# Gathers for experts 4 to 7 issued before the last store lands, and the weights of experts 6 and 7 loaded 1 MB at a time

## The chip, the cores and the metric

The kernel runs on one core of one Trainium2 chip. The metric is device time in microseconds (us), the median of several executions. Lower is better.

## The reference

The program is a linear attention followed by a mixture of experts with one expert per token. Cut to what matters:

```python
# q, k, v: (4, 8, 768, 64) float32;  gamma_h = 1 - 2 ** (-5 - h)
for t in range(S):
    state = gamma * state + outer(k[t], v[t])          # per batch and head
    y[t] = scale * q[t] @ state
x = y.transpose(0, 2, 1, 3).reshape(3072, 512)          # N tokens, D = 512
out = x
chosen = x @ w_skip > 0
e = argmax(x @ w_gate)                                  # one of 8 experts
y = softmax_weight * (relu(x @ w1[e]) @ w2[e])          # w1: 512 x 1024, w2: 1024 x 512
out[chosen] = x[chosen] + y[chosen]
```

All inputs and the output are float32. The kernel computes the expert products in bfloat16 and adds them up in float32.

## The kernel before

**Attention.** A loop over 16 pairs of heads, four for each of the four batches, computes the attention in chunked form (lines 540 to 610). The rows of batch b are put together in an SBUF tile `xall[b]`, which has two buffers, and stored to `out` in HBM. The last batch is stored in two steps, each on SP's and ACT's queue (lines 324 and 327). The gate of a batch (`g_logits` to `slots`) finds for each expert the tokens that go to it and writes their row numbers into slots. Slots 0 to 127 of every expert (s = 0, table `SL[0]`) are filled from batches 0 to 2 alone; slots 128 to 255 (s = 1, `SL[1]`) hold the rest and rows of the last batch.

**Experts.** A tile is a pair (e, s) of 128 tokens of one expert. For each tile the kernel does the following:
- `gather` (line 623): an indirect DMA on POOL reads the 128 rows out of `out` into a buffer `xg`, of which there are eight.
- `cast` (637): VectorE (DVE) casts them to bfloat16 (`xb`).
- `turn` (642): TensorE (PE) transposes them, and a copy brings them to SBUF (`xgT`).
- `layer1` (664): PE multiplies by `w1b[e]`, ACT applies the ReLU (`hT`).
- `second` (680): PE multiplies by `w2b[e]` into one of two PSUM buffers (`yps`).
- `give_back` (689): DVE computes `yo`, of which there are three buffers, and an indirect DMA on POOL scatters it to the rows of `out` (695).

**Weights.** `piece_w` (165) issues one piece of an expert's weights as a DMA on POOL, which casts from float32 to bfloat16: 512 KB read, 256 KB written, eight pieces per expert, `give(n)` issues the next n. Experts 0 to 4 have homes of their own and are loaded during the attention. The homes of experts 5 to 7 (pool `late`, line 718) take the place of the attention's tiles once these are released (717).

**Order.** All engines run the order written in the code. Each engine works its own list in order, so an instruction of POOL that waits holds up all that stands behind it, DMA issues included. After the attention, the first tiles of experts 0 to 3 are gathered (707), eight pieces of expert 5 are issued (722), and the first two tiles are computed while the gate of the last batch runs. Line 735 then gathers the second tiles of experts 0 to 3; these read rows of the last batch and wait for its store. From line 757 on, a loop goes over ten tasks: tiles (2,0), (3,0), (0,1) to (3,1) alone, then experts 4 to 7 with both tiles. In each round PE does layer 1 of task n, the transposes of task n + 1 and layer 2 of task n; DVE does the copy of n + 1, the cast of n + 2 and `yo` of n; POOL issues the scatters of n, then the gathers of `rows_of`, then pieces of `give`. After the scatters of round 6 POOL drains (769). A loop at the end (774) handles experts with more than 256 tokens and isn't entered with this input.

Of the kernel before, what the change touches and what calls it, by code (L numbers as in the profile page):

```python
# [9 lines left out]
FP32 = mybir.dt.float32  # L10
# [8 lines left out]
def kernel(  # L19
# [12 lines left out]
    PE, V_, A_, G_, SP = nc.tensor, nc.vector, nc.scalar, nc.gpsimd, nc.sync  # L32

    B, H, S, D = q.shape
    N, DM = out.shape
    E = moe_w1.shape[0]
# [10 lines left out]
    NST = CAP // 128  # L47
    NFIRST = 4
    NEARLY = 5
# [53 lines left out]
    for n in range(NIDLE):  # L103
        PE.matmul(
            out=idle[:, 0, :].rearrange("p (a c) -> p a c", a=4), lhsT=ones[:, :],
            rhs=ones[:, :].unsqueeze(1).to_broadcast([128, 4, 128]), start=True, stop=True,
# [34 lines left out]
    for r in range(R):  # L141
        for hi in range(2):
            G_.affine_select(
                out=maskc[64 * hi : 64 * hi + 64, r, :], in_=maskc[64 * hi : 64 * hi + 64, r, :],
# [14 lines left out]
    w1b, w2b = {}, {}  # L159

    def home_w(e, pl):
        w1b[e] = pl.tile([128, NDB, F], BF16, tag=f"w1_{e}", bufs=1, name="w1b")
        w2b[e] = pl.tile([128, NFB, DM], BF16, tag=f"w2_{e}", bufs=1, name="w2b")

    def piece_w(e, which, a):
        if which == 0:
            G_.dma_start(out=w1b[e][:, a, :], in_=moe_w1[e, a * 128 : (a + 1) * 128, :])  # L167
        else:
            G_.dma_start(  # L169
                out=w2b[e][:, 2 * a : 2 * a + 2, :].rearrange("p r d -> p (r d)"),  # L170
                in_=moe_w2[e, a * 256 : (a + 1) * 256, :].rearrange("(p r) d -> p (r d)", r=2),
            )
# [3 lines left out]
    pieces = [(e, w, a) for e in range(NEARLY) for w in range(2) for a in range(4)]  # L176

    def give(n):
        for _ in range(n):
            if pieces:  # L180
                piece_w(*pieces.pop(0))
# [179 lines left out]
    def g_turn(Gs):  # L361
        lp = wide("lps")
        for j in range(G):
            PE.transpose(out=lp[:, 0, j * 128 : (j + 1) * 128], in_=Gs[:, j * 128 : (j + 1) * 128], identity=ident[:, :])
        L = st("L", [128, NCH, 9])
        l4 = lp[:, 0, 0 : G * 128].rearrange("p (j c k e) -> p j c k e", j=G, c=2, k=2)
        half = st("half", [128, NCH, 9])
        V_.tensor_copy(half[:, :, :].rearrange("p (j c) e -> p j c e", c=2), l4[:, :, :, 0, 0:9])
        V_.tensor_tensor(
            out=L[:, :, :].rearrange("p (j c) e -> p j c e", c=2), in0=l4[:, :, :, 1, 0:9],  # L370
            in1=half[:, :, :].rearrange("p (j c) e -> p j c e", c=2), op=ALU.add,
        )
        return L
# [124 lines left out]
    gt, SL = {}, {}  # L498
# [41 lines left out]
    for i in range(NU + 1):  # L540
# [28 lines left out]
        if i == 1:  # L569

            identb = poolC.tile([128, 128], BF16, name="identb")
# [43 lines left out]
    poolE = ctx.enter_context(tc.tile_pool(name="esb", bufs=1, side="right", reuse_waits="tile"))  # L615
    xg, xgT, hTs = {}, {}, {}
    gathers, scatters = [], []

    def free_of(d, others):
        for o in others:  # L620
            tc.declare_no_dep(d.ins, o.ins, reason="the slots of a pass name distinct rows; rows of empty slots are not used")

    def gather(e, s, gi, upto, first=True):
        t = poolE.tile([128, DM], FP32, tag="xg", bufs=8, name="xg")
        d = G_.indirect_dma_start(  # L625
            out=t[:, :], out_offset=None, in_=out[0:upto, :],
            in_offset=bass.IndirectOffsetOnAxis(ap=gi[:, e : e + 1], axis=0), bounds_check=upto - 1, oob_is_err=False,
        )
        xg[e, s] = t
        if first:  # L630
            free_of(d, scatters)
            gathers.append(d)


    xbs = {}

    def cast(e, sts):
        for s in sts:
            xbs[e, s] = poolE.tile([128, DM], BF16, tag="xb", bufs=3, name="xb")
            V_.tensor_copy(xbs[e, s][:, :], xg[e, s][:, :])  # L640

    def turn(e, sts, copy=V_.tensor_copy):
        xgT[e] = poolE.tile([128, NDB, CAP], BF16, tag="xgT", bufs=3, name="xgT")
        for s in sts:
            ps = psum.tile([128, 2, 512], FP32, tag="P", bufs=2, name="xtp")
            pb = ps[:, 0, :].bitcast(BF16)
            for db in range(NDB):
                PE.transpose(
                    out=pb[:, db * 128 : (db + 1) * 128], in_=xbs[e, s][:, db * 128 : (db + 1) * 128], identity=identb[:, :]
                )  # L650
            copy(  # L651
                xgT[e][:, :, s * 128 : (s + 1) * 128], pb[:, 0 : NDB * 128].rearrange("p (a t) -> p a t", a=NDB)
            )

    tasks = [(2, [0]), (3, [0])] + [(e, [1]) for e in range(NFIRST)] + [(e, [0, 1]) for e in range(NFIRST, E)]
    todo = [(e, 1) for e in range(NFIRST)] + [(e, s) for e in range(NFIRST, E) for s in range(NST)]

    def rows_of(n):
        for _ in range(n):
            if todo:  # L660
                e, s = todo.pop(0)
                gather(e, s, SL[s][0], N)

    def layer1(e, sts):
        c0, n = sts[0] * 128, 128 * len(sts)
        hT = poolE.tile([128, NFB, CAP], BF16, tag="hT", bufs=2, name="hT")
        for f2 in range(NFB // 2):
            hp = psE.tile([128, 2, CAP], FP32, tag="hps", bufs=2, name="hps")
            for f in range(2):
                fb = 2 * f2 + f  # L670
                a, r = divmod(fb, 2)
                for db in range(NDB):
                    PE.matmul(  # L673
                        out=hp[:, f, 0:n], lhsT=w1b[e][:, db, a * 256 + r : (a + 1) * 256 : 2], rhs=xgT[e][:, db, c0 : c0 + n],
                        start=(db == 0), stop=(db == NDB - 1),
                    )
            A_.activation(out=hT[:, 2 * f2 : 2 * f2 + 2, 0:n], in_=hp[:, :, 0:n], func=AF.Relu, bias=0.0, scale=1.0)  # L677
        return hT
# [24 lines left out]
    def layer2(e, hT, sts, SL, first=False):  # L703
        for n, s in enumerate(sts):
            give_back(e, s, second(e, hT, n), SL, first)

    for e in range(NFIRST):
        gather(e, 0, SL[0][0], (B - 1) * S)
# [5 lines left out]
    Gs = g_cols(B - 1)  # L714
    t_x(NU - 1)
    turn(0, [0])
    stR.close()
    poolL = ctx.enter_context(tc.tile_pool(name="late", bufs=1, reuse_waits="tile"))
    for e in range(NEARLY, E):
        home_w(e, poolL)  # L720
    pieces += [(e, w, a) for e in range(NEARLY, E) for w in range(2) for a in range(4)]
    give(8)
    psE = ctx.enter_context(tc.tile_pool(name="pse", bufs=1, space=bass.MemoryType.PSUM, reuse_waits="tile"))
    L = g_turn(Gs)
    turn(1, [0])
    ha, pe = g_pick(L)
    h0 = layer1(0, [0])
    cp = g_count(B - 1, ha)
    g_vals(B - 1, ha, pe)
# [6 lines left out]
    cast(2, [0])  # L736
    give_back(0, 0, yp, SL, True)
    h0 = layer1(1, [0])
    turn(2, [0], A_.copy)
    cast(3, [0])  # L740
    layer2(1, h0, [0], SL, True)
# [4 lines left out]
    def passes():  # L746

        cn = g_count_all()
        top = poolC.tile([128, 1], FP32, name="top")
        V_.tensor_reduce(out=top[:, :], in_=cn[:, 0, 0:E], axis=AXX, op=ALU.max)  # L750
        V_.tensor_scalar(thr[:, :], thr[:, :], top[:, 0:1], None, ALU.is_lt)
        npass = poolC.tile([128, 1], FP32, name="npass")
        V_.tensor_reduce(out=npass[:, :], in_=thr[:, :], axis=AXX, op=ALU.add)
        V_.tensor_copy(npass_i[:, :], npass[:, :])

    give(4)
    for n, (e, sts) in enumerate(tasks):
        hT = layer1(e, sts)
        if n + 1 < len(tasks):
            turn(*tasks[n + 1])  # L760
        if n + 2 < len(tasks):
            cast(*tasks[n + 2])
        layer2(e, hT, sts, SL, True)
        rows_of(2 if n < 2 else 1)
        give(2)
        if n == 2:
            passes()
        if n == 6:
            G_.drain()
# [4 lines left out]
    with tc.For_i(0, n_more) as _:  # L774
        V_.tensor_scalar(posT[:, :], posT[:, :], -float(CAP), None, ALU.add)
        V_.memset(Tsb[:, :], 0.0)
        for b in range(B):
            slot_table(one_hots(poolE, chunks(b), every), chunks(b), every)
        SL2 = {s: slots(poolE, s, f"l{s}") for s in range(NST)}
        for e in range(E):  # L780
            for s in range(NST):
                gather(e, s, SL2[s][0], N, False)
            cast(e, [0, 1])
            turn(e, [0, 1])
            layer2(e, layer1(e, [0, 1]), [0, 1], SL2)
# [30 lines left out]
```

## Time and profile before

| | us |
|---|---|
| median of 3 runs | 221.69 |
| the runs | 222.35, 219.22, 221.69 |
| the profiled execution | 218.75 |
| its span, first to last instruction | 216.9 |

| engine | busy us | share of the span |
|---|---|---|
| PE, matmul | 190.7 | 88% |
| PE, weight load | 145.4 | 67% |
| POOL | 116.7 | 54% |
| DVE | 98.0 | 45% |
| ACT | 81.5 | 38% |

All times in the trace count from the first instruction. PE's matmul and weight load overlap and are listed apart. A hole is time in which an engine waits; the trace names what ended it. POOL's time for a DMA is that of its issue; the transfer lands later, and the time from issue to landing is listed by itself. The granted clock of PE was 0.992 of its full speed over the span, and 1.00 in every stretch of the experts' part up to the last product. DMA share is the mean busy share of the core's 16 DMA engines and can come out slightly over 1.

### The profile page before, as it was taken

The page shows a single profiled execution, that of the slowest core. Times are in us where ns is not written, and L with a number is a line of the kernel's source. Part 1 is how long each engine was busy: PE and PEld are TensorE (multiplying, and loading weights), DVE is VectorE, ACT ScalarE, POOL GpSimd, SP SyncE. Part 2 cuts the span into 40 slices and gives each one's busy share as a digit, 9 for nine tenths or more (in the row PEclk, how much of TensorE's full clock was granted, in tenths as well). Part 3 has the DMA queues.
Part 4 walks back from the last instruction along what each step waited for, and adds up shares of the span by engine and source line. Part 5 has one row for each costly group of instructions (what it writes and reads, how often), then busy time and mean ns, then how long its engine had stood idle before and what let it go on. Part 6 is the DMA issues. An engine that isn't in the chain of part 4 may idle for free. (4 is left out here: it accounts for less than half of the span.)

```text
span 216.9 us, 8067 instructions
## 1 busy us (share of the span) xinstructions
PE 190.7 (88%) x3516; PEld 145.4 (67%) x3516; DVE 98.0 (45%) x307; ACT 81.5 (38%) x156; POOL 116.7 (54%) x146
## 2 busy tenths in 40 slices
PE   6779999979988999988999987879999979999950
PEld 1668888756867886867886776566677657766710
DVE  4446435314773253664451676358335333334140
ACT  3344454433523633524444323343344224313400
POOL 4486457436174384461596701850488887860360
PEclk9999999999999999999999999999999999999996
DMA  6999999999999999999599999999969999994131
GB/s 186 292 255 296 281 229 269 275 237 317 263 308 256 268 259 250 286 306 219 158 193 187 236 271 224 265 271 226 215 228 153 259 275 232 204 207 118 48 137 38
DMA packets 54679, 49.88 MB, mean 230 GB/s; under 512 B 3834, under 2 KB 42362, under 8 KB 54640
## 3 DMA queue, kind: packets, MB, share of 16 engines
q0 software_dynamic: 11776, 24.07, 53.9%
q1 hardware_dynamic: 39648, 19.75, 34.8%
q10 hardware_dynamic: 3216, 5.51, 7.0%
q8 instruction: 29, 0.48, 0.9%
q14 instruction: 10, 0.08, 0.1%
HBM read 56.64 MB, written 10.49 MB: 309 GB/s over the span
## 5 line engine op out<-in xcount | busy, mean ns | idle before, releaser
L130 POOL TENSOR_TENSOR ks<-kw,tk 128x768 f32<-128x768 f32 x15 | 22.5, 1497 | 42.8 <-issue 39.7
L234 DVE TENSOR_TENSOR ATm<-atps,maskc 128x768 f32<-128x768 f32 x32 | 30.5, 953 | 23.6 <-PE atps L230 23.5
L677 ACT ACTIVATE hT<-hps 128x256 bf16<-128x256 f32 (+1 forms) x48 | 21.7, 454 | 38.7 <-PE hps L673 38.1
L230 PE MATMUL atps<-QT,KT 64*64 64x128 f32 x768 | 31.5, 275 | 3.8 <-issue 2.6
L673 PE MATMUL hps<-xgT,w1b 128*128 128x128 bf16 (+1 forms) x384 | 31.6, 237 | 2.4 <-DVE xgT L651 1.2
L673 PEld LDWEIGHTS <-w1b 128*128 128x128 bf16 x384 | 27.6, 97 | 7.3 <-issue 3.5
L683 PE MATMUL yps<-w2b,hT 128*128 128x512 bf16 x128 | 29.8, 379 | 0.4 <-DVE yo L692 0.4
L230 PEld LDWEIGHTS atps<-QT,KT 64*64 64x64 f32 x768 | 23.7, 133 | 6.9 <-issue 3.8
L294 PE MATMUL yps<-ATm,vw 64*64 64x128 f32 x768 | 25.9, 274 | 2.0 <-issue 1.1
L625 POOL DMA_INDIRECT xg<-out_dram,gi x16 | 16.6, 1039 | 20.2 <-DMA out_dram<-xall 16.0
L211 ACT COPY QT<-qtps 128x768 f32<-128x768 f32 x16 | 14.0, 876 | 34.4 <-PE qtps L192 34.4
L130 POOL TENSOR_TENSOR qs<-qw,tq 128x768 f32<-128x768 f32 x15 | 22.6, 1510 | 7.8 <-DMA qw<-in_q_dram 7.7
L294 PEld LDWEIGHTS yps<-ATm,vw 64*64 64x64 f32 x768 | 21.4, 133 | 5.2 <-issue 4.1
L695 POOL DMA_INDIRECT out_dram<-yo,si x16 | 16.6, 1038 | 14.5 <-issue 11.9
L692 DVE SCALAR_TENSOR_TENSOR yo<-yps,g,xg 128x512 f32<-128x512 f32 x16 | 11.9, 747 | 24.9 <-DMA out_dram<-yo,si 21.8
L169 POOL DMA_DIRECT2D w2b<-in_moe_w_dram x32 | 17.8, 567 | 7.1 <-DMA xg<-out_dram,gi 2.6
L683 PEld LDWEIGHTS <-hT 128*128 128x128 bf16 x128 | 12.0, 97 | 13.0 <-issue 0.9
L203 ACT COPY KT<-ktps 128x768 f32<-128x768 f32 x16 | 12.7, 796 | 19.1 <-PE ktps L192 19.1
L261 DVE COPY Z<-kvps 128x64 f32<-128x64 f32 x16 | 3.6, 223 | 33.8 <-PE kvps L251 33.8
L167 POOL DMA_DIRECT2D w1b<-in_moe_w_dram x32 | 17.9, 575 | 0.6 <-DMA w2b<-in_moe_w_dram 0.6
L300 ACT COPY xT<-yps 128x768 f32<-128x768 f32 x16 | 12.8, 800 | 13.3 <-PE yps L294 13.3
L251 PE MATMUL kvps<-vw,ks 64*64 64x64 f32 x640 | 15.0, 223 | 2.3 <-issue 2.3
(106 smaller groups left out, 237.1 us busy)
## 6 DMA issues: line engine op xcount, KB each, us to landing
w1b<-in_moe_w_dram POOLq DMA_DIRECT2D x32, 256.0 KB, 7.2
w2b<-in_moe_w_dram POOLq DMA_DIRECT2D x32, 256.0 KB, 7.7
qw<-in_q_dram SPq DMA_DIRECT2D x16, 384.0 KB, 6.7
kw<-in_k_dram SPq DMA_DIRECT2D x16, 384.0 KB, 7.9
vw<-in_v_dram SPq DMA_DIRECT2D x16, 384.0 KB, 6.6
out_dram<-xall ACTq DMA_DIRECT2D x6, 512.0 KB, 6.5
out_dram<-xall ACTq DMA_DIRECT2D x1, 1536.0 KB, 17.0
out_dram<-xall SPq DMA_DIRECT2D x1, 576.0 KB, 6.1
```

Source lines behind the costliest of these rows:

```text
L130: eng.tensor_tensor(o[i][:, :, :, :], in_, sc, ALU.mult)
L167: G_.dma_start(out=w1b[e][:, a, :], in_=moe_w1[e, a * 128 : (a + 1) * 128, :])
L169: G_.dma_start(out=w2b[e][:, 2 * a : 2 * a + 2, :].rearrange("p r d -> p (r d)"), in_=moe_w2[e, a * 256 : (a + 1) * 256, :].rearrange("(p ...
L230: PE.matmul(out=ps[cp, h, g * C : (g + 1) * C], lhsT=KT[i][hp, r, g, cp], rhs=qcols(i, 2 * g + c)[hp], start=True, stop=True,)
L234: V_.tensor_tensor(out=ATm[i, r][:, :, :, :], in0=ps[:, :, 0 : G * C].rearrange("p h (g t) -> p h g t", g=G), in1=maskc[:, r, :].unsqueeze ...
L251: PE.matmul(out=ps[64 * h : 64 * h + 64, c, g * D : (g + 1) * D], lhsT=ks[i][cp, R * g + r, h, :], rhs=vw[i][cp, h * G + g, r * D : (r + 1 ...
L294: PE.matmul(out=Y[i][home(h, c), c, g * C : (g + 1) * C], lhsT=vw[i][cp, h * G + g, r * D : (r + 1) * D], rhs=ATm[i, r][cp, h, g, :], star ...
L625: d = G_.indirect_dma_start(out=t[:, :], out_offset=None, in_=out[0:upto, :], in_offset=bass.IndirectOffsetOnAxis(ap=gi[:, e : e + 1], axi ...
L673: PE.matmul(out=hp[:, f, 0:n], lhsT=w1b[e][:, db, a * 256 + r : (a + 1) * 256 : 2], rhs=xgT[e][:, db, c0 : c0 + n], start=(db == 0), stop= ...
L677: A_.activation(out=hT[:, 2 * f2 : 2 * f2 + 2, 0:n], in_=hp[:, :, 0:n], func=AF.Relu, bias=0.0, scale=1.0)
L683: PE.matmul(out=yp[:, :], lhsT=hT[:, fb, n * 128 : (n + 1) * 128], rhs=w2b[e][:, fb, :], start=(fb == 0), stop=(fb == NFB - 1),)
L695: sc = G_.indirect_dma_start(out=out[:, :], out_offset=bass.IndirectOffsetOnAxis(ap=si[:, e : e + 1], axis=0), in_=yo[:, :], in_offset=Non ...
```

## The change

The first tiles of experts 4 to 7 (s = 0) are gathered right after the eight pieces of expert 5, ahead of the line that gathers the second tiles of experts 0 to 3. They don't use the eight buffers of `xg`: each has a tile of its own in pool `late`, allocated behind the weights of experts 5 to 7. `rows_of` issues four gathers fewer in the task loop, one per round in rounds 0 to 3. The weights of experts 6 and 7 are loaded in two pieces per matrix instead of four, each with 1 MB read and 512 KB written, so that each partition takes 2 (w1) or 4 (w2) neighbouring rows; `give` hands out half as many. As the rows of w1 now lie in another order over the partitions, the transposes and the weight loads of these two experts pick their columns with other steps (`rows_in`): the transposes by 2 instead of 1, the loads of w1 by 4 instead of 2.

```diff
     def piece_w(e, which, a):
-        if which == 0:
+        if e > NEARLY:
+
+            t, src, m = (w1b[e], moe_w1, 2) if which == 0 else (w2b[e], moe_w2, 4)
+            G_.dma_start(
+                out=t[:, m * a : m * a + m, :].rearrange("p r c -> p (r c)"),
+                in_=src[e, a * 128 * m : (a + 1) * 128 * m, :].rearrange("(p r) c -> p (r c)", r=m),
+            )
+        elif which == 0:
             G_.dma_start(out=w1b[e][:, a, :], in_=moe_w1[e, a * 128 : (a + 1) * 128, :])
...
-    def gather(e, s, gi, upto, first=True):
-        t = poolE.tile([128, DM], FP32, tag="xg", bufs=8, name="xg")
+    def gather(e, s, gi, upto, first=True, home=None):
+        t = poolE.tile([128, DM], FP32, tag="xg", bufs=8, name="xg") if home is None else home
...
+    def rows_in(j, m):
+
+        a, r = divmod(j, m)
+        return slice(128 * m * a + r, 128 * m * (a + 1), m)
...
-                    out=pb[:, db * 128 : (db + 1) * 128], in_=xbs[e, s][:, db * 128 : (db + 1) * 128], identity=identb[:, :]
+                    out=pb[:, db * 128 : (db + 1) * 128],
+                    in_=xbs[e, s][:, rows_in(db, 1 if e <= NEARLY else 2)],
+                    identity=identb[:, :],
...
-    todo = [(e, 1) for e in range(NFIRST)] + [(e, s) for e in range(NFIRST, E) for s in range(NST)]
+    todo = [(e, 1) for e in range(E)]
...
-                a, r = divmod(fb, 2)
                 for db in range(NDB):
                     PE.matmul(
-                        out=hp[:, f, 0:n], lhsT=w1b[e][:, db, a * 256 + r : (a + 1) * 256 : 2], rhs=xgT[e][:, db, c0 : c0 + n],
+                        out=hp[:, f, 0:n], lhsT=w1b[e][:, db, rows_in(fb, 2 if e <= NEARLY else 4)],
+                        rhs=xgT[e][:, db, c0 : c0 + n],
...
-    pieces += [(e, w, a) for e in range(NEARLY, E) for w in range(2) for a in range(4)]
+    pieces += [(e, w, a) for e in range(NEARLY, E) for w in range(2) for a in range(4 if e == NEARLY else 2)]
     give(8)
+
+    for e in range(NFIRST, E):
+        gather(e, 0, SL[0][0], (B - 1) * S, home=poolL.tile([128, DM], FP32, tag=f"xh_{e}", bufs=1, name="xh"))
...
-    give(4)
+    give(2)
...
-        rows_of(2 if n < 2 else 1)
-        give(2)
+        rows_of(1)
+        give(1)
```

## Rows read from the trace of the kernel before

**Rows 1.** Stretches: length, busy us (count) of PE, PEld, DVE, ACT, POOL, clock, DMA.

```profile
146.70:154.00 7.30, 7.28 (x77) 4.73 (x73) 5.23 (x24) 2.41 (x7) 0.05 (x2) 1.00 1.13 224
154.00:158.00 4.00, 3.92 (x48) 2.85 (x46) 0.93 (x4) 1.55 (x5) 3.09 (x4) 1.00 0.95 211
158.00:161.60 3.60, 3.51 (x42) 2.45 (x39) 1.92 (x4) 1.46 (x4) 2.99 (x4) 1.00 0.70 249
161.60:193.90 32.30, 30.73 (x292) 21.68 (x290) 12.79 (x29) 10.91 (x24) 26.46 (x33) 1.00 1.02 222
...
199.70:203.30 3.60, 3.37 (x24) 2.24 (x24) 1.50 (x4) 0.51 (x1) 0.00 (x0) 1.00 0.00 0
```

**Rows 2.** Timeline of PE: start, duration, line, operation, count, idle before and releaser.

```profile
157.22 2.19 PE L673 MATMUL hps<-xgT,w1b 128*128 128x128 bf16 x32
159.26 0.39 PE L648 MATMUL xtp<-identb,xb 128*128 128x128 bf16 x4
...
178.78 3.69 PE L673 MATMUL hps<-xgT,w1b 128*128 128x256 bf16 x32 [1.24 <-DVE xgT L651]
...
199.93 1.89 PE L683 MATMUL yps<-w2b,hT 128*128 128x512 bf16 x8 [0.44 <-DVE yo L692]
...
205.18 3.66 PE L683 MATMUL yps<-w2b,hT 128*128 128x512 bf16 x16
```

**Rows 3.** Timeline of DVE.

```profile
158.62 0.56 DVE L640 CAST xb<-xg 128x512 bf16<-128x512 f32 x1 [2.50 <-DMA xg<-out_dram,gi]
...
177.31 0.75 DVE L692 SCALAR_TENSOR_TENSOR yo<-yps,g,xg 128x512 f32<-128x512 f32 x1 [3.45 <-DMA out_dram<-yo,si]
177.98 0.74 DVE L651 COPY xgT<-xtp 128x512 bf16<-128x512 bf16 x2
...
208.88 0.75 DVE L692 SCALAR_TENSOR_TENSOR yo<-yps,g,xg 128x512 f32<-128x512 f32 x1 [0.82 <-PE yps L683]
```

**Rows 4.** Timeline of POOL.

```profile
144.61 0.54 POOL L169 DMA_DIRECT2D w2b<-in_moe_w_dram  x1 [1.55 <-DMA xg<-out_dram,gi]
146.19 0.53 POOL L169 DMA_DIRECT2D w2b<-in_moe_w_dram  x1 [1.05 <-DMA xg<-out_dram,gi]
153.97 1.05 POOL L625 DMA_INDIRECT xg<-out_dram,gi  x1 [7.25 <-DMA out_dram<-xall]
...
169.58 1.04 POOL L695 DMA_INDIRECT out_dram<-yo,si  x1 [0.30 <-issue]
...
203.31 0.98 POOL L695 DMA_INDIRECT out_dram<-yo,si  x1 [9.42 <-issue]
...
209.91 0.98 POOL L695 DMA_INDIRECT out_dram<-yo,si  x1 [0.46 <-DVEq L774]
```

**Rows 5.** us to landing of the issues at 144.61, 146.19, 153.97, 169.58, 209.91.

```profile
w2b<-in_moe_w_dram POOLq DMA_DIRECT2D x1, 256.0 KB, 12.2
...
w2b<-in_moe_w_dram POOLq DMA_DIRECT2D x1, 256.0 KB, 11.7
...
xg<-out_dram,gi POOLq DMA_INDIRECT x1, 4.6
...
out_dram<-yo,si POOLq DMA_INDIRECT x1, 7.6
...
out_dram<-yo,si POOLq DMA_INDIRECT x1, 3.5
```

**Rows 6.** POOL's groups from 153.9 to 193.9: count, busy us, mean ns, idle before.

```profile
L625 POOL DMA_INDIRECT xg<-out_dram,gi x12 | 12.5, 1043 | 10.6 <-DMA out_dram<-xall 7.3 <-issue 3.4
...
L169 POOL DMA_DIRECT2D w2b<-in_moe_w_dram x8 | 4.8, 613 | 0.0
L167 POOL DMA_DIRECT2D w1b<-in_moe_w_dram x8 | 4.6, 593 | 0.6 <-DMA w2b<-in_moe_w_dram 0.6
```

**Rows 7.** Weight loads of PE over 140 to 210, shapes apart: count, busy us, mean ns.

```profile
L673 PEld LDWEIGHTS <-w1b 128*128 128x128 bf16 x384 | 27.6, 97 | 7.3 <-issue 3.5
L683 PEld LDWEIGHTS <-hT 128*128 128x128 bf16 x128 | 12.0, 97 | 13.0 <-issue 0.9
```

## The prediction

> **What bounds the kernel now.** I read the table of stretches first, then the timelines of PE, DVE and POOL from 139 us to the end, then the landings of single transfers. From 149 us to 208.8 us PE is all but closed. Of that part the 3.6 us from 158 to 161.6 hold 3.51 us of PE work [rows 1], and the timeline shows two holes of any size: 1.24 us ahead of expert 4's first layer at 178.78, and 0.44 us at 199.93 [rows 2]. The first ends when DVE copies xgT at 177.98. That copy stood behind a yo that began at 177.31, after 3.45 us of waiting for a scatter [rows 3]: yo has three buffers, and the scatter that frees this one, (3,0), was issued at 169.58 [rows 4] and took 7.6 us to land [rows 5], thus 177.2. The last scatter of the program lands in 3.5 us [rows 5]; the difference is the queue ahead of it. From 161.6 to 193.9 us the DMA engines are full (1.02), while from 199.7 to 203.3 they carry nothing [rows 1].
>
> So PE sets the end, and through yo the DMA ring sets PE's one large hole. The end itself: PE's last second layer ends at 205.18 + 3.66 = 208.84 [rows 2], yo begins at 208.88 and takes 0.75 [rows 3], its scatter is issued at 209.91 [rows 4], and the program closes at 216.9. What PE gains or loses before 208.8 goes one for one into the end, unless POOL becomes the later of the two: its six last scatters run from 203.31, so by 1.29 us each it would issue the last at 203.31 + 5 x 1.29 = 209.76 even without yo, against 209.91 as it was [rows 4].
>
> **The four gathers that move.** On POOL they leave the stretch 153.9 to 193.9, where a gather costs 1.04 us [rows 6] and the 0.3 us ahead of it, 4 x 1.34 = 5.4 us in all. They go behind the last piece of expert 5's weights at 146.19, into the 7.25 us in which POOL waits for the last store [rows 4]. They fit: 5.4 us of 7.25. Each transfer of POOL waits for the one eight before it to land (the piece at 144.61 is held by the third gather, eight back [rows 4]), so the new gathers wait for pieces 1 to 4 of expert 5. Piece 7 landed at 144.61 + 12.2 = 156.8 and piece 8 at 146.19 + 11.7 = 157.9, 1.1 us apart [rows 4, 5]; three such steps before 156.8, piece 4 is down by about 153.5. The last new gather can then hold POOL to about 154.5, some 0.6 us past the store. That half microsecond lies under what follows.
>
> Their homes cost no wait. By the sizes in the code, the attention pool has 45,600 bytes per partition ahead of xall (QT 9,216, KT 6,144, ATm 12,288, Z 2,560, seen with padding 32, xT 15,360). The late pool starts at the same place and puts three experts' weights (49,152) before the homes. These cover 49,152 to 57,344, inside xall's first buffer (up to 57,888), which batch 2 used; the store in flight reads the second.
>
> In the ring they cost something. Piece 8 lands at 157.9, and the gather of tile (0,1), issued four microseconds earlier at 153.97, lands at 153.97 + 4.6 = 158.6 [rows 4, 5]: it had queued behind the weights and came 0.7 us after them. DMA share is 1.13 and 0.95 up to 158 us [rows 1], so nothing idle takes the new gathers in. They stand between piece 8 and gather (0,1). One costs 0.7 us by that step, or half of a piece's 1.1 us (it reads half the bytes), 0.55; I take 0.65, thus 4 x 0.65 = 2.6 us. DVE is already waiting for (0,1): its cast begins at 158.62, after 2.50 us for this gather [rows 3], and PE's transposes of it at 159.26 [rows 2], 0.08 us after the cast ends. PE's work before them runs to 157.22 + 2.19 = 159.41 [rows 2]. So nearly all of the 2.6 us becomes a hole of PE: **+2.5 us**. Bounds: 0 (ring not in order) and 4 x 0.7 + 0.6 = 3.4. I take the value next to the row of gather (0,1), which shows this very queue.
>
> **The 1 MB pieces.** Sixteen pieces of experts 6 and 7 become eight. A piece costs POOL 0.59 to 0.61 us [rows 6], so 8 x 0.6 = 4.8 us go if a doubled piece costs POOL the same, and nothing if it costs double (no row has one). Either way it is off the path: neither hole of PE is ended by w1b or w2b [rows 2]. The Trainium skill (DMA: Bandwidth & Descriptors, section Anatomy of one DMA) gives each transfer of this kind a fixed 2.0 us beside the time of its bytes; by it eight transfers fewer would give an estimated 16 us back to the ring. Here two pieces in a full ring land 1.1 us apart with all their bytes [rows 5], so no such part is paid per piece, and I take 0 for it.
>
> **The yo waits.** Up to the scatter (3,0) the ring gets four gathers more and one fewer, (4,0), so 3 x 0.65 = 2.0 us of work is added; from 158 to 161.6 it had 0.30 x 3.6 = 1.1 us free [rows 1]. At worst, then, that scatter lands at 177.2 + 2.0 - 1.1 = 178.1 instead of 177.2. At best it comes earlier than before: POOL, busy 26.46 of 32.3 us from 161.6 on [rows 1], loses up to 10.2 us of issues, so it stops being what holds scatters back. Before, PE went on 178.78 - 177.31 = 1.47 us after that yo began [rows 2, 3]; at worst it could now do so at 178.1 + 1.47 = 179.6. But behind the hole at 159 it arrives only at 177.54 + 2.5 = 180.0 (177.54 is where the old hole begins [rows 2]). The hole is gone in either case, by 0.4 us at worst: **-1.24 us**. At 199.93 the same reasoning holds with more room: PE arrives 2.5 - 1.24 = 1.3 us later, and by then the other three gathers too have left the ring's work: **-0.44 us**. What is late next is the gather (0,1) alone. The POOL wait of 9.42 us before 203.31 is the drain at line 769 [rows 4]; with its scatters out no later it ends no later, while PE's end comes later, so POOL's 209.76 stays covered.
>
> **Strided weights.** Experts 6 and 7 read w1 at a step of 4 columns instead of 2 (64 loads), and 16 transposes read xb at a step of 2. A load at step 2 takes 97 ns, the same as the unstrided one of hT [rows 7]; a first-layer matmul of 256 columns has 3.69 / 32 = 115 ns [rows 2]. At 97 the load stays hidden: 0. If the step doubled it, 64 x (194 - 115) = 5.1 us. I take 0, since contiguous to 2 cost nothing.
>
> **Sum.** +2.5 - 1.24 - 0.44 = +0.8 us against the profiled execution, 218.75 us (span 216.9 and 1.85 around it): 219.6. That execution stands 2.9 us under the median of the runs shown, 221.69 (219.22 to 222.35). On the median the forecast is 221.69 + 0.8 = **222.5 us**.
>
> **Rivals.**
> First, faster: gather (0,1) isn't held up. For it: the ring is only 0.70 full from 158 to 161.6 [rows 1], so engines that finish early could take the new gathers while the slowest is still at piece 8. Against: a landing counts the slowest engine, and that one has them all ahead. It gives -1.7 us, 220.0.
> Second, slower: the loads of w1 at step 4. The place is the first layers of experts 6 and 7, it decides from 115 ns per load on, and its price is up to 5.1 us over the forecast, 227.6, past the 2% line at 226.1. For it: no row has a step of 4. Against: step 2 is free [rows 7]. The Trainium skill (SBUF — State Buffer, section Door 1, the box on cachelines) lets bf16 step up to 8 for free; this would leave the forecast as it is, and no run here shows it yet.
> Third: the yo waits stay, because a doubled piece is slower in the ring than two, and the scatters behind it land later. Three doubled pieces stand ahead of scatter (3,0), so 0.13 us on each would use up the 0.4 us of the worst case. Then +2.5 us with nothing back: 224.2.
> Fourth: the change doesn't do what it says, and the new gathers wait for the last store after all. Gather (0,1) is then issued 5.4 us later, at 159.4, and lands after the 3.5 us of an empty ring [rows 5], at 162.9: a hole near 4.2 us, less 1.7, thus 224.2. The layout speaks against it.
>
> **How the numbers follow.** Forecast 0.52, first rival 0.24, second 0.07, third 0.11, fourth 0.04, unforeseen 0.02. The three runs shown lie 3.1 us apart, so each case gets about 1.5 us on either side. From 218.4 to 225.0 lie almost all of the forecast, the first rival but its fast edge, and most of the third and fourth: about 0.8. A measurement of this kernel can tell about 2%, 4.4 us. Slower by more: the second rival and the edge of the third and fourth, 0.11. Faster by more needs under 217.3: the edge of the first rival, 0.08. Within: 0.81.
>
> **What would show it.** In the changed profile, four gathers on POOL between 147 and 154 us; gather (0,1) landing near 161 and DVE's cast of it waiting some 5 us; a hole of about 2.5 us on PE ahead of its transposes at 159.4; none ahead of expert 4's first layer; w1b loads of experts 6 and 7 still at 97 ns. If the cast of (0,1) begins before 159.5, the first step is wrong; if PE still has a hole ahead of expert 4's first layer, the second is. A wait of PE for weights anywhere would make the whole wrong.

## The result, and the profile after

The changed kernel takes 221.44 us (median of 20 runs, 218.86 to 225.96), the kernel before 219.47 beside it (20 runs, 216.82 to 222.86). The ratio is 1.0068 with an interval of 1.0039 to 1.0097, so the change costs 1.5 us (0.9 to 2.1); the forecast was +0.8. Ratios here leave disturbed runs out, so they aren't quite the quotients of the medians. The profiled execution lies well under the median: 218.86 us, with a span of 217.1 and a mean clock of 0.982 (before: 218.75, 216.9 and 0.992).

Timeline of PE in the changed kernel (start, duration, line, operation, count, idle before and its releaser); line 660 is the transposes, 686 layer 1, 697 layer 2, 320 the attention's last transposes:

```profile
142.10 0.87 PE L320 MATMUL xps<-ident,xT 128*128 128x128 f32 x6
...
158.09 2.20 PE L686 MATMUL hps<-xgT,w1b 128*128 128x128 bf16 x32
161.88 0.40 PE L660 MATMUL xtp<-identb,xb 128*128 128x128 bf16 x4 [1.59 <-DVE xb L647]
162.11 1.89 PE L697 MATMUL yps<-w2b,hT 128*128 128x512 bf16 x8
163.84 2.20 PE L686 MATMUL hps<-xgT,w1b 128*128 128x128 bf16 x32
...
180.02 3.69 PE L686 MATMUL hps<-xgT,w1b 128*128 128x256 bf16 x32
...
205.82 3.62 PE L697 MATMUL yps<-w2b,hT 128*128 128x512 bf16 x16
```

One hole, ahead of the transposes of (0,1). The holes at expert 4's first layer and at 199.93 [rows 2] are gone: the row at 180.02 carries no bracket. DVE and POOL of the same kernel show what the hole waits for (cast of (0,1); then the last piece of expert 5, the four early gathers into `xh`, the gather of (0,1), and two scatters at the end):

```profile
161.39 0.43 DVE L647 CAST xb<-xg 128x512 bf16<-128x512 f32 x1 [4.40 <-DMA xg<-out_dram,gi]
```

```profile
146.61 0.53 POOL L176 DMA_DIRECT2D w2b<-in_moe_w_dram  x1 [2.77 <-DMA xg<-out_dram,gi]
147.68 1.06 POOL L632 DMA_INDIRECT xh<-out_dram,gi  x1 [0.53 <-DMA w1b<-in_moe_w_dram]
149.05 1.05 POOL L632 DMA_INDIRECT xh<-out_dram,gi  x1 [0.31 <-DMA w1b<-in_moe_w_dram]
150.81 1.00 POOL L632 DMA_INDIRECT xh<-out_dram,gi  x1 [0.71 <-DMA w1b<-in_moe_w_dram]
152.56 0.99 POOL L632 DMA_INDIRECT xh<-out_dram,gi  x1 [0.75 <-DMA w1b<-in_moe_w_dram]
154.59 1.00 POOL L632 DMA_INDIRECT xg<-out_dram,gi  x1 [1.04 <-DMA w2b<-in_moe_w_dram]
...
198.22 0.98 POOL L709 DMA_INDIRECT out_dram<-yo,si  x1 [7.73 <-issue]
...
210.50 0.98 POOL L709 DMA_INDIRECT out_dram<-yo,si  x1 [0.74 <-DVEq L791]
```

The last piece lands 11.4 us after its issue, at 146.61 + 11.4 = 158.0 (landing row below); DVE gets tile (0,1) at 161.39, 3.4 us later. In the kernel before that distance was 0.7. The difference, 2.7 us, is the four gathers in between (the other early traces, below, repeat it). DVE waits 4.40 us, yet PE only 1.59, for in this execution the attention ended 0.67 us later (142.10 against 141.43) and PE came to the place later with it.

The landing of the piece issued at 146.61 (KB written, us):

```profile
w2b<-in_moe_w_dram POOLq DMA_DIRECT2D x1, 256.0 KB, 11.4
```

Weight loads of w1 (count, busy us, mean ns), first over expert 4's first layer (180 to 183.5, step 2), then over expert 7's (202.2 to 205.8, step 4):

```profile
L686 PEld LDWEIGHTS <-w1b 128*128 128x128 bf16 x31 | 3.0, 98 | 0.5
...
L686 PEld LDWEIGHTS <-w1b 128*128 128x128 bf16 x31 | 3.4, 113 | 0.1
```

A load at step 4 takes 113 ns, 15 more than at step 2. A product in this layer has 115, so the layer still takes 3.69 us; the room left is 2 ns.

To compare executions whose attention ended at different times I use the **tail**: from the start of PE's last attention transposes (line 320) to the end of its last product. It was 208.84 - 141.43 = 67.4 us before and is 205.82 + 3.62 - 142.10 = 67.3 here. So this execution shows no loss at all, while the median says 1.5 us. What the others pay had to come from other executions.

### The profile page after: what moved, and what is told of

The parts are those of the page before. It is cut to its first block, busy times and chain, and to the rows that moved or that the text cites. A ratio compares the mean times of both kernels' runs of the same rounds, so it can differ in the third digit from the quotient of the medians.

```text
span 217.1 us, 8056 instructions
## 1 busy us (share of the span) xinstructions
PE 191.0 (88%) x3516; PEld 147.2 (68%) x3516; DVE 97.7 (45%) x307; ACT 81.5 (38%) x156; POOL 111.8 (51%) x138
## 5 line engine op out<-in xcount | busy, mean ns | idle before, releaser
L237 PE MATMUL atps<-QT,KT 64*64 64x128 f32 x768 | 32.4, 279 | 3.1 <-issue 1.4
L686 PEld LDWEIGHTS <-w1b 128*128 128x128 bf16 x384 | 28.4, 100 | 5.2 <-issue 2.0
L237 PEld LDWEIGHTS atps<-QT,KT 64*64 64x64 f32 x768 | 24.5, 135 | 5.8 <-issue 2.7
L632 POOL DMA_INDIRECT xg<-out_dram,gi x12 | 12.3, 1025 | 13.5 <-DVE g L499 7.6
L258 PE MATMUL kvps<-vw,ks 64*64 64x64 f32 x640 | 15.5, 224 | 4.3 <-issue 4.3
L210 ACT COPY KT<-ktps 128x768 f32<-128x768 f32 x16 | 12.7, 796 | 16.2 <-PE ktps L199 16.2
L258 PEld LDWEIGHTS kvps<-vw,ks 64*64 64x64 f32 x640 | 13.0, 135 | 7.6 <-issue 7.2
L176 POOL DMA_DIRECT2D w2b<-in_moe_w_dram x24 | 13.3, 586 | 7.7 <-DMA xg<-out_dram,gi 2.8
L199 PE MATMUL qtps<-ident,qs 128*128 128x128 f32 x96 | 14.4, 288 | 2.3 <-DVE L L376 1.1
```

Of the source, the lines that this page charges most:

```text
L176: G_.dma_start(out=w2b[e][:, 2 * a : 2 * a + 2, :].rearrange("p r d -> p (r d)"), in_=moe_w2[e, a * 256 : (a + 1) * 256, :].rearrange("(p ...
L199: PE.transpose(out=ps[:, r, g * 128 : (g + 1) * 128], in_=w[:, R * g + r, :, :].rearrange("p h d -> p (h d)"), identity=ident[:, :],)
L237: PE.matmul(out=ps[cp, h, g * C : (g + 1) * C], lhsT=KT[i][hp, r, g, cp], rhs=qcols(i, 2 * g + c)[hp], start=True, stop=True,)
L258: PE.matmul(out=ps[64 * h : 64 * h + 64, c, g * D : (g + 1) * D], lhsT=ks[i][cp, R * g + r, h, :], rhs=vw[i][cp, h * G + g, r * D : (r + 1 ...
L686: PE.matmul(out=hp[:, f, 0:n], lhsT=w1b[e][:, db, rows_in(fb, 2 if e <= NEARLY else 4)], rhs=xgT[e][:, db, c0 : c0 + n], start=(db == 0), ...
```

## The experiments

They went out in five groups, each on one chip with runs of the kernel before beside it. The kernel before had medians of 220.5 and 220.6 us in two of the groups and 230.8 to 231.7 in three. I call these **early** and **late** groups, by what their traces show: from the issue of expert 5's first piece to the issue of the gather of (0,1), which waits for the last store, it takes 14.2 to 15.9 us in the traces of early groups and 16.2 to 18.5 in those of late ones. In a late group the attention and its store come later against the weights, and the ring has more time to empty. The same chip was in a late group and then in an early one; why, I don't know. One thing in the traces parts the two kinds: from 100 us on, each of the twelve late ones has waits of ACT or DVE, the longest 2.8 to 7.9 us, that the profile puts down to `remote`, to nothing it shows on this core, and none of the eight early ones has any. The kernel before in the first group (DVE):

```profile
164.56 0.42 DVE L651 COPY xgT<-xtp 128x512 bf16<-128x512 bf16 x1 [2.83 <-remote]
```

What ends these waits stays open. The result above belongs to the early kind (14.2 before, 14.8 after).

### First group (late): the parts by themselves

Only the pieces, without the early gathers:

```diff
-    for e in range(NFIRST, E):
-        gather(e, 0, ..., home=...)
-    todo = [(e, 1) for e in range(E)]
+    todo = [(e, 1) for e in range(NFIRST)] + [(e, s) for e in range(NFIRST, E) for s in range(NST)]
-        rows_of(1)
+        rows_of(2 if n < 2 else 1)
```

> The 1 MB pieces alone, all gathers where they were. Ring theory (the four early gathers hold up the gather of tile (0,1)): no hole of PE ahead of the transposes of (0,1); up to eight issues of 0.6 us fewer on POOL; the holes ahead of expert 4's first layer (1.24 us) and at the second layer (0.44 us) shrink or stay, so -0.2 to -1.7 us against before, ratio 0.992 to 0.999. Pieces theory (the doubled pieces are what costs): about +1.5 us, ratio 1.007, like the whole change, and weight loads over 97 ns or scatters that land later.

Measured: 231.93 us against 231.62, ratio 0.9959 (0.9907 to 1.0011).

Only the gathers: 512 KB pieces and the old steps.

```diff
-        if e > NEARLY:
+        if False:
...
-    give(2)
+    give(4)
-        give(1)
+        give(2)
```

> The four early gathers alone, weights of experts 6 and 7 in 512 KB pieces as before. Ring theory: the whole loss is here: a hole of 1.6 to 2.5 us ahead of the transposes of (0,1), none ahead of expert 4's first layer, ratio 1.003 to 1.010. Pieces theory: no loss, ratio at or under 1.000.

Measured: 230.33 us, ratio 0.9822 (0.9733 to 0.9911). This ratio rests on two of its six runs; the medians alone give 0.994.

The swap: two pieces of expert 5, as many bytes as the four gathers read, are held back behind the gathers (0,1) to (3,1).

```diff
-    give(8)
+    give(6)
...
-        give(1)
+        give(2 if n == 0 else 1)
```

> The change, but the last two of expert 5's eight 512 KB pieces are held back until behind the gathers of tiles (0,1) to (3,1): the same 1 MB that the four early gathers read is taken out of the ring ahead of them. Ring theory: the gather of (0,1) lands at 158 to 158.6 instead of 161.3, no hole ahead of its transposes, and the holes at expert 4 and after stay away: -1.7 us against before, ratio 0.992, and 2.5 us or so under the change. If something other than ring order makes the change slow (homes, lanes, doubled pieces), the ratio stays near 1.007.

Measured: 228.75 us, ratio 0.98 (0.9741 to 0.9859).

The kernel before once more, for a trace:

> The kernel before, a second execution with a profile, to see how firm the two holes are that were credited. If they are part of the kernel: 1.24 us ahead of expert 4's first layer and 0.44 us at the second layer of expert 6, within some tenths. If they come and go: sum under 0.8 us, and the loss of the change is then the new hole with less to set against it.

Measured: 231.54 us. In its trace (POOL, then a stretch) the gather of (0,1) is issued at 160.94, after 12.72 us of waiting for the store, and the DMA engines are only 0.21 busy from 160 to 164 us: there is no full ring that an early gather could hold up.

```profile
160.94 1.06 POOL L625 DMA_INDIRECT xg<-out_dram,gi  x1 [12.72 <-DMA out_dram<-xall]
```

```profile
160.00:164.00 4.00, 3.92 (x45) 2.73 (x43) 1.06 (x3) 1.34 (x4) 2.45 (x3) 1.00 0.21 68
```

The holes that were asked for aren't in this trace: PE comes to expert 4's first layer, at 192.41, without a wait. Here the gathers gain (1.8% by the ratio, 0.6% by the medians) and the pieces nothing that can be told from zero, the reverse of the result. So these four runs couldn't speak for it, and the next group repeats them.

### Second group (early): the same comparison where the loss occurs

> The change itself, on another occasion. Ring theory, with a condition: the early gathers cost what they add to the ring only where the last store lands before expert 5's last piece (153.7 against 157.9 us in the first trace). There: hole of 1.5 to 2.5 us ahead of the transposes of (0,1), ratio 1.004 to 1.010. Where PE drops to half clock near 140 us and the store lands after 158 us, the ring is empty by then, the early gathers are through, and the change must come out at or under 0.99. Rival (the change is slow in itself: doubled pieces, homes, lanes): over 1.004 in either case.

Measured: 220.59 us against 220.52, ratio 1.0039 (0.9979 to 1.0099), which by itself can't be told from 1. Its trace shows what the first one lacked. PE's timeline, then stretches (length, busy us and count of PE, PEld, DVE, ACT, POOL, clock, DMA share, GB/s):

```profile
156.56 2.19 PE L686 MATMUL hps<-xgT,w1b 128*128 128x128 bf16 x32
161.48 0.61 PE L660 MATMUL xtp<-identb,xb 128*128 128x128 bf16 x4 [2.73 <-DVE xb L647]
161.88 3.00 PE L697 MATMUL yps<-w2b,hT 128*128 128x512 bf16 x8
164.72 2.20 PE L686 MATMUL hps<-xgT,w1b 128*128 128x128 bf16 x32
```

```profile
158.00:160.00 2.00, 0.75 (x14) 0.58 (x11) 0.00 (x0) 0.80 (x3) 1.39 (x3) 1.00 0.95 350
160.00:162.00 2.00, 0.52 (x5) 0.52 (x6) 1.00 (x2) 0.00 (x0) 1.70 (x2) 0.68 0.73 264
162.00:164.00 2.00, 2.00 (x6) 0.64 (x5) 0.84 (x3) 0.00 (x0) 1.69 (x4) 0.50 0.54 178
164.00:166.00 2.00, 1.92 (x23) 1.42 (x22) 0.75 (x1) 0.57 (x2) 1.70 (x2) 0.97 1.03 145
```

The hole is 2.73 us, about as forecast (2.5). Behind it the granted clock is at 0.50, 1.2 GHz in place of 2.4, for some 3 us, and the transposes and layer 2, which take 0.23 + 1.73 us from start to start in the first trace (161.88 to 163.84), take 0.40 + 2.84 here. That is 1.28 us on top of the hole. The tail is 69.5 us, 2.1 more than before: 2.73 + 1.28 - 1.68 (the two old holes) = 2.3.

The parts by themselves once more:

> The 1 MB pieces alone, again. Ring theory: no hole ahead of the transposes of (0,1), 0.992 to 0.999. Rival (doubled pieces cost): 1.004 to 1.010.

Measured: 219.30 us, ratio 1.0021 (0.997 to 1.0073): the pieces alone change nothing that can be measured. In its trace the large hole that the early gathers were to remove stands again, 1.30 us at expert 4's first layer. The one of 0.44 us doesn't; there is one of 0.30 us a round ahead of expert 4 instead (PE):

```profile
177.32 2.19 PE L686 MATMUL hps<-xgT,w1b 128*128 128x128 bf16 x32 [0.30 <-DVE xgT L665]
...
182.99 3.69 PE L686 MATMUL hps<-xgT,w1b 128*128 128x256 bf16 x32 [1.30 <-DVE xgT L665]
```

The swap, as above:

> As before: two pieces of expert 5 held back behind the gathers of (0,1) to (3,1). Ring theory: no hole ahead of the transposes of (0,1) where the clock is whole, 0.990 to 0.994 of before, and 1.2 to 1.8% under the change in the same call. Rival: within 0.5% of the change.

Measured: 219.17 us, ratio 0.9924 (0.9856 to 0.9993), 1.1% under the change (0.9924 / 1.0039). Its tail is 65.6 us, 1.8 less than before. The gather of (0,1), and DVE's cast of it:

```profile
156.90 1.00 POOL L632 DMA_INDIRECT xg<-out_dram,gi  x1 [5.09 <-DMA out_dram<-xall]
```

```profile
160.23 0.50 DVE L647 CAST xb<-xg 128x512 bf16<-128x512 f32 x1 [1.06 <-DMA xg<-out_dram,gi]
```

The gather lands within 3.3 us of its issue, and PE has no hole of 0.3 us or more after 152 us. With no new hole, the old ones' 1.68 us remain as a gain: -1.8 in the tail, -1.7 in the ratio (0.0076 x 220.5).

Two early gathers in place of four:

```diff
-    for e in range(NFIRST, E):
+    for e in range(NFIRST, NFIRST + 2):
...
-    todo = [(e, 1) for e in range(E)]
+    todo = [(e, 1) for e in range(6)] + [(6, 0), (6, 1), (7, 0), (7, 1)]
-        rows_of(1)
+        rows_of(2 if 0 < n < 3 else 1)
```

> The change with two early gathers (experts 4 and 5) instead of four; those of 6 and 7 go back into the task loop. Ring theory: half the work ahead of (0,1), 1.3 us: the cast of (0,1) begins 1.3 us earlier against expert 5's last landing than with four, the hole is near 0.9 us or less, and the later holes are still covered: ratio 0.996 to 1.002, between the change and before or under both. Rival: as the change.

Measured: 218.26 us, ratio 0.9962 (0.9915 to 1.001), tail 66.0. The hole shrinks and the old ones stay away (PE):

```profile
162.12 0.40 PE L660 MATMUL xtp<-identb,xb 128*128 128x128 bf16 x4 [0.46 <-DVE xb L647]
```

From the tail, half the gathers leave 0.46 of hole, no half clock (1.00 from 158 to 170 us), and the whole credit: 0.46 - 1.68 = -1.2, measured -1.4.

The early traces together show what one gather costs in the ring. The measure is again the time from the landing of expert 5's last piece to DVE's cast of (0,1). Without early gathers in between, only_pieces_again has 0.7 to 0.8 us (piece issued at 150.03, landed 11.2 us later), as the kernel before had 0.7. With two it is 2.0 (148.43, landed 11.2 us later). With four it is 3.3 to 3.4, in the first trace and in the three others, one of them with filling products. The casts, of only_pieces_again and of the two gathers:

```profile
161.98 0.43 DVE L647 CAST xb<-xg 128x512 bf16<-128x512 f32 x1 [2.17 <-DMA xg<-out_dram,gi]
```

```profile
161.58 0.48 DVE L647 CAST xb<-xg 128x512 bf16<-128x512 f32 x1 [3.21 <-DMA xg<-out_dram,gi]
```

That is 0.6 to 0.7 us for each gather, as forecast.

### Third and fourth group (late): filling the hole

If the clock falls because PE idles, work put into the hole should keep it up. Eleven products that nobody reads go where PE waits for (0,1):

```diff
         hT = layer1(e, sts)
+        if n == 1:
+            fill = psum.tile([128, 2, 512], FP32, tag="P", bufs=2, name="fill")
+            for _ in range(11):
+                PE.matmul(out=..., lhsT=ones[:, :], rhs=..., start=True, stop=True)
```

> The change with eleven products of ones (512 columns, about 0.22 us each at full clock, result not used) put on PE between layer 1 of tile (3,0) and the transposes of (0,1), so that PE works where it would wait. Clock theory: the hole costs more than its length because PE comes out of it at half clock (0.50 at 162 to 164 us in the change's second trace, 1.3 us lost). Then the clock stays 1.00 from 158 to 168 us here, the transposes of (0,1) start no later, and the stretch from PE's last attention transposes to its last product is 68.2 us or less where the change took 69.5; ratio 0.999 to 1.003, under the change by 0.3 to 0.6%. Rival (only the hole's length counts): no difference from the change, or slower by what the filling runs over.

Measured: 232.69 us against 230.75, ratio 1.0147 (1.0001 to 1.0293); inconclusive, because on this occasion the hole isn't where the products are.

> The change again, in the same call as the filled hole. Clock theory: a hole over 2.5 us ahead of the transposes of (0,1) is followed by half clock and a stretch from the last attention transposes to the last product of 69 us or more; a hole under 2 us by full clock and 67.5 us. Rival: full clock after the hole whatever its length.

Measured: 229.16 us, ratio 0.9963 (0.9888 to 1.0037). Its trace has no hole ahead of the transposes of (0,1), so it tells neither theory from the other.

> The kernel before, one more profile. Credit theory: holes of 1.0 to 1.4 us ahead of expert 4's first layer and of some tenths at expert 6's second layer, from the last attention transposes to the last product 67.4 us within 0.5. Rival (the credit was an accident of one execution): no such holes and about 65.7 us.

Measured: 230.85 us; the gather of (0,1) starts at 162.68 us. A miss: there is no hole ahead of expert 4's first layer, and the tail is 70.7 us. The trace also has a hole of 2.21 us after which layer 2 takes its full-clock time of 1.89 us (PE; the clock is 1.00 from 171.7 to 176):

```profile
171.75 0.61 PE L673 MATMUL hps<-xgT,w1b 128*128 128x128 bf16 x8 [2.21 <-ACT hT L677]
...
172.41 1.89 PE L683 MATMUL yps<-w2b,hT 128*128 128x512 bf16 x8
```

The early gathers ahead of expert 5's pieces:

```diff
+    for e in range(NFIRST, E):
+        gather(e, 0, ..., home=...)
     give(8)
-
-    for e in range(NFIRST, E):
-        gather(e, 0, ..., home=...)
```

> The change with the four early gathers ahead of expert 5's eight pieces instead of behind them. Ring theory: what counts is the work in the ring ahead of the gather of (0,1), and that is the same: its cast begins within 0.7 us of the change's against the start of the pieces, a hole of 2 to 3 us, ratio 1.002 to 1.010. Rival (the waits of the early gathers on POOL for the eighth transfer back hold things up): they no longer wait there, so the hole shrinks by 1 us or more.

Measured: 236.15 us, ratio 1.0373 (1.0232 to 1.0514), a miss for every theory. POOL issued the gathers from 141.21 us on, PE ran at 0.50 from 140 to 155, its last attention transposes started at 154.63 (147.09 in the changed kernel of this group), and the store landed at 166.6. Whether the order does this to the attention or only met it isn't settled.

The fourth group repeats the filled kernel, the changed one and the swap with the kernel before:

> The change with the hole ahead of the transposes of (0,1) filled by eleven products of ones, once more: the first time PE had been at half clock since 138 us and the last store came late, so the hole was another one. Clock theory, where PE is whole up to 158 us: clock 1.00 from 158 to 168 us, the stretch from the last attention transposes to the last product 67 to 68.2 us, 0.3 to 0.6% under the change. Rival (length alone counts): no difference from the change, or slower.

> The change, in the same call. Clock theory: a hole of 2.5 us or more ahead of the transposes of (0,1), clock 0.5 to 0.7 in the 2 us after it, from the last attention transposes to the last product 69 us or more, ratio 1.003 to 1.010. Rival: clock 1.00 after the hole.

> The kernel before where PE is whole up to 158 us. Credit theory: holes of 1.0 to 1.4 us ahead of expert 4's first layer and some tenths at expert 6's second layer, 67.4 us from the last attention transposes to the last product. Rival (accident of one execution): none, and 65.7 us.

> Two pieces of expert 5 held back, as the version to keep: ratio 0.990 to 0.996 and the shortest of the call; no hole ahead of the transposes of (0,1) nor later. Rival: no better than before.

Measured against 231.66 us: filled 232.43, ratio 0.9908 (0.9861 to 0.9955), which rests on four of its 13 runs while its median is the higher one; changed 229.93, ratio 0.9857 (0.9809 to 0.9904); swap 230.60, ratio 0.9862 (0.98 to 0.9925); before 229.5. The group is late again, so it says nothing of the filling, but it confirms the sign: in late groups the change gains. The swap is no better than the change here. The kernel before misses its forecast again, with a tail of 73.2 us and no hole ahead of expert 4's first layer. Its largest hole on PE, and the stretches around it:

```profile
166.86 1.01 PE L673 MATMUL hps<-xgT,w1b 128*128 128x128 bf16 x8 [3.00 <-issue]
```

```profile
164.00:168.00 4.00, 1.01 (x8) 0.85 (x8) 0.22 (x1) 0.54 (x2) 3.39 (x6) 0.78 0.63 234
168.00:172.00 4.00, 3.72 (x18) 2.12 (x18) 0.82 (x2) 0.88 (x3) 3.08 (x4) 0.50 1.01 147
```

Half clock behind a hole stands here too, in the kernel before.

### Fifth group (early): the filled kernel beside the changed one

> The changed kernel with eleven products of ones (into a PSUM tile of their own, read by nothing) put on TensorE behind step (0, 1)'s predecessor, where it waits for the gather of (0, 1). If the last store lands ahead of e5's pieces (near 154 us): theory (the hole's length plus half clock behind it): no stretch at 0.50 behind the hole, and a time 0.5 to 1.3 us below the changed kernel's of the same call. Rival (the length alone counts): the same time within 0.4 us, or up to 0.7 us above it where the products outlast the hole. If the last store lands near 160 us the hole isn't there, and the run tells nothing.

> The changed kernel once more, beside the filled one on the same chip. Theory: 0.3 to 0.7% above the kernel before where the last store lands near 154 us, 0.4 to 1.5% below it where it lands near 160 us. Rival (the change costs the same everywhere): 0.3 to 0.7% above it in either case.

Measured against 220.55 us: filled 222.54 (6 runs, no ratio), changed 222.43, ratio 1.0048 (0.9997 to 1.01). By the medians the rival holds: filling brings nothing. The traces of the stretch say otherwise. The changed kernel (PE, then stretches):

```profile
155.89 2.19 PE L686 MATMUL hps<-xgT,w1b 128*128 128x128 bf16 x32
...
159.87 2.20 PE L686 MATMUL hps<-xgT,w1b 128*128 128x128 bf16 x32
163.75 0.46 PE L660 MATMUL xtp<-identb,xb 128*128 128x128 bf16 x4 [1.68 <-DVE xb L647]
164.00 3.55 PE L697 MATMUL yps<-w2b,hT 128*128 128x512 bf16 x8
167.39 2.20 PE L686 MATMUL hps<-xgT,w1b 128*128 128x128 bf16 x32
```

```profile
162.00:164.00 2.00, 0.32 (x7) 0.26 (x5) 0.74 (x2) 0.42 (x2) 1.69 (x2) 0.99 0.81 268
164.00:166.00 2.00, 2.00 (x8) 0.74 (x6) 1.01 (x3) 0.00 (x0) 1.76 (x3) 0.50 0.56 215
166.00:168.00 2.00, 2.00 (x15) 1.05 (x14) 0.41 (x1) 0.00 (x0) 1.63 (x2) 0.66 1.04 141
```

The filled kernel:

```profile
162.57 2.19 PE L686 MATMUL hps<-xgT,w1b 128*128 128x128 bf16 x32
164.60 2.54 PE L779 MATMUL fill<-onesb 128*128 128x512 bf16 x11
167.05 0.40 PE L660 MATMUL xtp<-identb,xb 128*128 128x128 bf16 x4
167.28 1.89 PE L697 MATMUL yps<-w2b,hT 128*128 128x512 bf16 x8
169.01 2.19 PE L686 MATMUL hps<-xgT,w1b 128*128 128x128 bf16 x32
```

```profile
164.00:166.00 2.00, 2.00 (x21) 1.29 (x19) 0.00 (x0) 0.82 (x3) 1.70 (x2) 1.00 0.98 367
166.00:168.00 2.00, 2.00 (x14) 0.90 (x12) 1.51 (x4) 0.00 (x0) 1.70 (x3) 1.00 0.71 266
```

```profile
166.49 0.49 DVE L647 CAST xb<-xg 128x512 bf16<-128x512 f32 x1 [5.03 <-DMA xg<-out_dram,gi]
```

From one first layer to the next PE needs 3.98 us where nothing waits (155.89 to 159.87). Around the hole it needs 7.52 unfilled (159.87 to 167.39), so 3.54 too much: 1.68 of hole, 1.68 of half clock (0.25 + 3.39 from 163.75 to 167.39 in place of 0.23 + 1.73), and 0.18 of draining. Filled it needs 6.44, 2.46 too much, and the clock stays at 1.00: layer 2 takes 1.89 us again. Yet (0,1) came no sooner: its cast ends at 166.98, so without the products PE would have stood still from 164.76 (162.57 + 2.19) to 167.05, 2.29 us, longer than the 1.68 of the changed kernel. The stretch is 1.08 us shorter all the same, and the tail is 67.8 instead of 68.9. One filled trace against three unfilled ones, of which one kept its clock by itself, supports the filling as the cause but doesn't prove it. That the medians don't show it I can only bound: the filled kernel's profiled attention ended 2.7 us later (146.79 against 144.07), with clocks of 0.91 at 20 to 40 and 60 to 80 us, and such drifts are larger than what is sought. What is shown, then, is the clock behind the hole in the traces, not its share of the medians. One number recorded for every run points the same way, the mean granted clock of PE: 0.982 for the change against 0.985 before in the second group (12 and 35 runs), 0.979 against 0.984 in the fifth (12 and 17). Some 3 us at 0.50 out of 218 would take off 0.007. Single runs of one kernel spread by about 0.005, so this is a hint and no measurement of the share.

## Why the prediction was right or wrong, by its steps

**The gathers on POOL** went where they were put, 147.68 to 153.55, each released by the landing of an earlier piece. Right; the fourth rival is out.

**The queue in the ring** was put at 4 x 0.65 = 2.6 us; the first trace gives 3.4 - 0.7 = 2.7. Right, and the first rival (gather (0,1) not held up) is out. That it is the work in the ring ahead of gather (0,1) is shown by the swap, where as many bytes are taken away, and by the row of 0, 2 and 4 gathers: 0.7 to 0.8, 2.0, and 3.3 to 3.4 us.

**"So nearly all of the 2.6 us becomes a hole of PE: +2.5 us"** is the step that failed. The length it gives the hole was right or too long: three traces have 2.73, 1.68 and 1.59 us. In the two short ones the attention ended later against the weights (expert 5's first piece was issued 2.7 and 2.3 us ahead of PE's last attention transposes, against 1.5 us with the hole of 2.73 and 1.7 in the kernel before). But its price isn't its length. In two of three traces PE's clock fell to 0.50 behind it, for another 1.28 and 1.68 us; in the first it stayed at 1.00. The sum with this term is 2.5 + 1.3 (or 1.7) - 1.68 = +2.1 to 2.5 us where the hole has its forecast length, and 1.68 + 1.68 - 1.68 = +1.7 in the fifth group's trace (its tail: +1.5); without it, -0.1 in the first trace. The median's +1.5 (0.9 to 2.1) lies between; how often the half clock comes, and so its share of the +1.5, isn't shown. Why it came behind 1.68 us and not behind 1.59 stays open too. The trace before could not give this price: its clock is 1.00 in every stretch of the experts' part [rows 1], where PE's longest hole is 1.24 us [rows 2]. I took that 1.00 for granted behind a hole twice as long.

**The yo waits**: -1.24 and -0.44, right in the early traces: both holes are gone in all six with early gathers. Of the two without, the first has both and only_pieces_again the large one (1.30). The swap, which has this term alone, gains 1.7 us. The third rival is out. The late traces of the kernel before don't have these holes, so there is nothing of this kind to gain there.

**The doubled pieces**: taken as 0 off the path; only_pieces_again gives 1.0021. A doubled piece costs POOL about 0.6 us like a single one (POOL is busy 111.8 us instead of 116.7, 4.9 less, against 4.8 expected). The estimate of 16 us back to the ring misread the fixed 2.0 us of the Trainium skill (DMA: Bandwidth & Descriptors, section Anatomy of one DMA): the same section says that it is mostly the latency of completion. The run agrees: eight transfers fewer changed no time that can be measured (1.0021).

**The strided loads**: right in the time, wrong in the step. A load at step 4 costs 113 ns instead of 97, not nothing; it is hidden by 2 ns. The Trainium skill (SBUF — State Buffer, section Door 1, the box on cachelines) has bf16 free up to a step of 8; the trace does not agree, and the measurement decides.

**The median as a base** was high by chance: 221.69 from three runs, 219.47 from twenty. That made the forecast time (222.5) too high by more than the change was priced too low.

**What it missed altogether**: the sign goes with the kind of group, in which the last store lands early or late against the weights; that the store's time is the cause isn't shown. In late groups the changed kernel gains 1.4% (0.9857; 0.7% by the medians) or can't be told from 1 (0.9963). There the ring runs nearly empty while the kernel before waits for the store (0.21 in its first late trace), and neither late trace of the changed kernel has a hole ahead of the transposes of (0,1). Which instructions hand the gain on isn't settled.

## What to carry to other kernels

In this kernel a transfer put early into a full ring was paid by the next one behind it that somebody waited for. Keep the ring's bytes ahead of that one constant, by moving as many bytes back as you move forward. The swap does this and beat the kernel before in all three groups it ran in (0.98, 0.9924, 0.9862); the changed kernel it beat where the ring was full (1.0039) and equalled where it wasn't (0.9857). A hole of PE in a stretch at full clock must be priced twice, at its length alone and with half clock behind it.

## What the runs showed of the hardware

- PE's clock fell to 0.50 behind holes of 2.73 and 1.68 us and not behind one of 1.59, all at the same place with the same work around, and came back within 4 us. Elsewhere it fell behind one of 3.00 and not behind one of 2.21, so length alone doesn't decide.
- Each gather of 256 KB issued ahead of gather (0,1) in a full ring moved its landing by 0.6 to 0.7 us.
- Weight loads of bf16 take 97 to 98 ns at steps 1 and 2, and 113 at step 4.
- The same kernel on the same chip had medians of 231.66 us in one group and 220.55 in a later one.
